# Linear attention with a gated product behind it: key features as the stationary side, and k of two heads projected in PSUM

## The chip, the cores and the metric

The kernel runs on one core of a Trainium2 chip. The metric is the device time of one execution in microseconds (us); the median of repeated runs counts.

## The reference

`phi` maps each token of a head (64 numbers) to 256 features; the attention is linear in them. Its output, with all heads of a token side by side, goes through two weight matrices whose products are multiplied, and through a third. q, k, v and w_phi are float32, the other three weights float64.

```python
# q, k, v: 8 batches, 8 heads, 576 tokens, 64 numbers; w_phi: 64 x 128
def phi(x):
    proj = np.einsum('bhsd,df->bhsf', x, w_phi)
    proj = proj - np.max(np.abs(proj), axis=-1, keepdims=True)
    return np.concatenate([np.exp(proj), np.exp(-proj)], axis=-1)
q_p, k_p = (phi(q), phi(k))
kv = np.einsum('bhsf,bhsd->bhfd', k_p, v)
z = np.sum(k_p, axis=2)
num = np.einsum('bhsf,bhfd->bhsd', q_p, kv)
den = np.einsum('bhsf,bhf->bhs', q_p, z)[..., None] + 1e-06
x = (num / den)               # then heads side by side: 4608 tokens x 512
a = x @ w_a                   # 512 x 1536
b = x @ w_b
return a * b @ w_out          # 1536 x 512
```

## The kernel before, in words

**Two parts that run woven into each other.** The attention goes over 32 pairs of heads (8 batches of 4 pairs; pair i is `b, pr = divmod(i, 4)`). The product behind it (called MoE in the names) goes over blocks of 288 tokens with the first 6 of 12 slices of the inner width (`moe_block`, lines 565 and 588), and then in a second pass over blocks of 512 tokens with the other six (`second_pass`, lines 648 and 695). `attention_steps` gives each stage of a pair a turn by a table of numbers (`K_TURNS`, `KV_TURN`, `Q_TURNS` and so on), and between turns `run` puts in steps of MoE blocks whose input is ready. Each tile comes from a pool with a fixed number of buffers, and the framework then sets the order of instructions on each engine and the waits.

**Precision.** An f32 matmul is slow, and an fp32r matmul rounds its inputs. So most products are made of split operands: a high part (rounded to fp32r) and a low part (what is left), and `products` multiplies high by high, high by low and low by high. The first pairs use plain f32 matmuls instead, which need no splitting by VectorE and ScalarE: `PLAIN_K` is the pair from which k is split for its projection, `PLAIN_KV` that from which the features and v are split, `PLAIN_NUM` and `PLAIN_Q` the same for the numerator and the queries.

**The keys of a pair.** `k_load` and `rest_load` fetch k and v: 512 tokens of two heads as four chunks of 128 tokens, and the remaining 64 tokens of two pairs together as one "rest" chunk. For plain pairs `features` multiplies a chunk (both heads' 64 numbers on 128 partitions) with `wk32`, a block-diagonal `w_phi` of 256 columns, into one tile `pk`. For split pairs k is loaded twice, so that each head's high part and low part lie one under the other on 128 partitions (`ks`, made by `stack`); one matmul per head with `wk2` of 256 columns (high `w_phi` twice, and its low part beside it) then gives two halves of `pk` that have to be added: ScalarE copies one half to `kb`, VectorE adds the other into `kd` (lines 236 and 237). VectorE takes the maximum (239) and subtracts it (240), ScalarE makes both exponentials `ke`, and `split` makes `keh` and `kel`.

**Sum over the tokens.** `kv_add` (line 292) accumulates v's transposed product with the features over all chunks in `kvps`: v with a column of ones is the stationary side (65 columns: `vaug` is v's high part with the ones, `vl` its low part), the features of one head (256 columns) are the moving side. In split pairs that is three matmuls per head and chunk. `k_finish` copies the sum (`kvT`), turns it by four TensorE transposes into `pt` (314), and makes `kvh` and `kvl`, which `q_side` uses for the numerators `pn` (370).

**PSUM.** The eight banks: three for the MoE (`ps_moe`), four that `pk`, `pq` (queries' projection) and `pn` share (`att`), one for `kvps` and `pt` (`kvacc`; batch 0 uses a bank of the MoE's).

Of the kernel before, what the change touches and what calls it, by code (L numbers as in the profile page):

```python
# [10 lines left out]
F32 = mybir.dt.float32  # L11
# [26 lines left out]
PLAIN_K, PLAIN_Q, PLAIN_KV, PLAIN_NUM = 9, 9, 11, 9  # L38
# [4 lines left out]
    "k_lo": "vvv",  # L43
    "v_hi": "sss",
# [15 lines left out]
def tile_kernel(ctx, tc, qT, km, kr, vm, vr, w_phi, w_a, w_b, w_out, out):  # L60
# [23 lines left out]
    TS = (HALF, T2)  # L84
    NFS = (SLICES0, DF // P - SLICES0)
# [25 lines left out]
    def attention_consts(a1):  # L111
# [7 lines left out]
        wk32 = a1.tile([P, 2, F], F32, tag="rk", name="wk32")  # L119
        nc.vector.memset(wk32, 0.0)  # L120
        for j in range(2):
            rows = slice(j * D, (j + 1) * D)
            nc.vector.tensor_copy(wk32[rows, j, :], w2[rows, :])
        wk2 = a1.tile([P, 2, F], F32R, name="wk2")
        nc.vector.memset(wk2.bitcast(F32), 0.0)
        nc.vector.tensor_copy(wk2[:, 0, :], wh)
        nc.vector.tensor_copy(wk2[:D, 1, :], wl[:D])
# [28 lines left out]
    def k_load(b, pr, a1, a2, ps, consts, st):  # L156
# [4 lines left out]
        if i < PLAIN_K:  # L161
            k32 = a1.tile([P, n], F32, tag="ks", bufs=2, name=f"k32_{u}")
            nc.sync.dma_start(k32, km[b, pr])
        else:
            k32 = a1.tile([P, 2, n], F32, tag="k32", name=f"k32_{u}")
            for r in range(2):
                nc.sync.dma_start(k32[r * D : (r + 1) * D], km[b, pr].rearrange("(j d) s -> d j s", j=2))
        if i < PLAIN_KV:
            v32 = a1.tile([P, NFULL, 2, D + 1], F32, tag="vl", bufs=2, name=f"v32_{u}")
            nc.vector.memset(v32[:, :, :, D : D + 1], 1.0)  # L170
        else:
            v32 = a1.tile([P, NFULL, 2, D], F32, tag="v32", name=f"v32_{u}")
# [3 lines left out]
        if i >= PLAIN_K:  # L176
            ks = a1.tile([P, 2, n], F32R, tag="ks", bufs=2, name=f"ks_{u}")
            stack(ks, k32, engine("k_hi", b), engine("k_lo", b))
            st["k", b, pr] = (ks,)
        yield  # L180
        st["v", b, pr] = (v32,)
        if i >= PLAIN_KV:
            va = vaug[pr % 2]
            vl = a1.tile([P, NFULL, 2, D + 1], F32R, tag="vl", bufs=2, name=f"vl_{u}")
            split(va[:, :, :, :D], vl[:, :, :, :D], v32, engine("v_hi", b), engine("v_lo", b))
            st["v", b, pr] = (va, vl)
        yield

    def rest_load(b, g, a1, a2, ps, consts, st):
# [3 lines left out]
        if i < PLAIN_K:  # L193
            k32 = a1.tile([P, P], F32, tag="rk32", name=f"rk32_{u}")
            nc.sync.dma_start(k32, kr[b, g])
        else:
            k32 = a1.tile([P, 2, P], F32, tag="rk32", name=f"rk32_{u}")
            for r in range(2):
                nc.sync.dma_start(k32[r * D : (r + 1) * D], kr[b, g].rearrange("(j d) s -> d j s", j=2))
# [17 lines left out]

    def features(u, i, k_, c0, n, a2, ps, consts):

        wk32, wk2 = consts[3:5]  # L220
        d = a2.tile([P, 4, F], F32, tag="kd", bufs=1, name=f"kd_{u}")[:, : 2 * n]
        if i < PLAIN_K:
            pk = ps.tile([P, 2, 2 * F], F32, tag="att", name=f"pk_{u}")
            for c in range(n):
                nc.tensor.matmul(pk[:, c], k_[:, (c0 + c) * P : (c0 + c + 1) * P], wk32, start=True, stop=True)
            p = pk[:, :n].rearrange("p c (j f) -> p (c j) f", j=2)
        else:

            p = d
            kb = a2.tile([P, 4, F], F32, tag="kb", bufs=1, name=f"kb_{u}")  # L230
            for c in range(n):
                pk = ps.tile([P, 2, 2, F], F32, tag="att", name=f"pk_{u}_{c}")
                for j in range(2):
                    nc.tensor.matmul(pk[:, j], k_[:, j, (c0 + c) * P : (c0 + c + 1) * P], wk2, start=True, stop=True)  # L234
                to = slice(2 * c, 2 * c + 2)
                nc.scalar.copy(kb[:, to], pk[:, :, 1])
                nc.vector.tensor_tensor(d[:, to], pk[:, :, 0], kb[:, to], op=ALU.add)
# [20 lines left out]
    def k_chunks(b, pr, c0, a1, a2, ps, consts, st):  # L258

        u = f"{b}_{pr}"  # L260
        gen = features(f"{u}_{c0}", b * NPAIR + pr, st["k", b, pr][0], c0, 2, a2, ps, consts)
# [23 lines left out]
    def kv_add(b, pr, vs, es, st):  # L285

        left = st["kv_left", b, pr] = st["kv_left", b, pr] - 1
        for j in range(2):
            parts = products(vs, es)
            for n_, (v_, e_) in enumerate(parts):  # L290
                width = D if n_ == 2 else D + 1
                nc.tensor.matmul(  # L292
                    st["kv_ps", b, pr][:width, j],
                    v_[:, j, :width],
                    e_[:, j],
                    start=(left == NFULL and j == 0 and n_ == 0),
                    stop=(left == 0 and n_ == len(parts) - 1),
                    skip_group_check=True,
                )

    def spare(b, ps):

        return (ps_moe, "moe", 3) if b == 0 else (ps, "kvacc", 1)

    def k_finish(b, pr, a1, a2, ps, consts, st):
# [3 lines left out]
        kvT = a2.tile([P, 4, F], F32, tag="kb", bufs=1, name=f"kvT_{u}")  # L309
        nc.scalar.copy(kvT[: D + 1], st["kv_ps", b, pr][: D + 1].rearrange("p j (s f) -> p (j s) f", s=2))  # L310
        pool, tag, bufs = spare(b, ps)
        pt = pool.tile([P, 4, P], F32, tag=tag, bufs=bufs, name=f"pt_{u}")
        for g in range(4):
            nc.tensor.transpose(pt[:, g, : D + 1], kvT[: D + 1, g, :], ident[: D + 1, : D + 1])
# [527 lines left out]
```

## Time and profile before

| | |
|---|---|
| median of 3 runs | 1260.65 us (1260.07 to 1265.03) |
| span of the profiled execution | 1260.6 us |
| TensorE busy | 1229.8 us (98%) |
| weight loads busy (beside matmuls) | 1131.8 us (90%) |
| VectorE busy | 928.8 us (74%) |
| ScalarE busy | 734.3 us (58%) |
| GpSimd busy | 157.3 us (12%) |
| mean granted TensorE clock | 0.998 |

How to read the profile: PE is TensorE's matmul, PEld its weight load, which runs beside matmuls, DVE is VectorE, ACT ScalarE, POOL GpSimd, SP the queue that issues DMAs. A group's row gives line, engine, operation, output and inputs by the program's names, the shape (for a matmul "128*65 128x256": 128 partitions by 65 stationary columns, 256 moving columns), how often, busy us and mean ns of one, and then idle time before it with what ended it. A row of the timeline gives start, length and the group. The matmuls of the split pairs are fp32r though the rows print "f32".

### The profile page before, as it was taken

Reading aid. Unit: us, or ns where it says so; the run is one execution under the profiler, and the core shown is the slowest. Engines: PE = TensorE matmul, PEld = TensorE weight load, DVE = VectorE, ACT = ScalarE, POOL = GpSimd, SP = SyncE. Lnnn points to the kernel's source line nnn. Section 1 sums busy time; section 2 is a strip of 40 time slices with the busy share of each in tenths; the row PEclk is TensorE's granted clock in tenths of the full one; section 3 lists DMA queues with packets and bytes.
Section 4 is the critical chain, followed back from the end, with each engine's and each line's share of the span. In section 5 each row is a group of like instructions: output and inputs, shape, how many; then the busy total and the mean of one; then the engine's idle time right before and its main releaser. Section 6 shows DMA issues by size and latency. Waiting matters only on the chain.

```text
span 1260.6 us, 22965 instructions
## 1 busy us (share of the span) xinstructions
PE 1229.8 (98%) x8588; PEld 1131.8 (90%) x8588; DVE 928.8 (74%) x1682; ACT 734.3 (58%) x1577; POOL 157.3 (12%) x70
## 2 busy tenths in 40 slices
PE   7889999999999999999999999999999999999998
PEld 4556789899999999999999999999999999999997
DVE  6989658898898989989974983599556556456443
ACT  5766668788888889988885542454223223233221
POOL 2232221221222212221220000000000000000000
PEclk9999999999999999999999999999999999999999
DMA  7665443443444435344233561142432332331221
GB/s 188 174 182 154 117 125 90 108 128 103 122 110 123 127 101 141 81 129 130 62 82 104 166 204 58 46 146 83 125 94 70 107 101 67 101 103 51 66 68 50
DMA packets 126287, 138.24 MB, mean 110 GB/s; under 512 B 39712, under 2 KB 92448, under 8 KB 126176
## 3 DMA queue, kind: packets, MB, share of 16 engines
q1 hardware_dynamic: 126176, 136.78, 38.4%
q8 instruction: 67, 1.10, 0.4%
q14 instruction: 44, 0.36, 0.1%
HBM read 108.12 MB, written 28.61 MB: 108 GB/s over the span
## 4 chain that ended last, share of the span: by engine, by line
PE 76%; DVE 9%; DMA 6%; ACT 5%; issue 2%; SPq 1%; POOL 0%; DVEq 0%; ACTq 0%
PE pab L648 21%; PE po L695 11%; PE pa L565 10%; PE pb L565 10%; PE po L588 9%; PE kvps L292 6%; PE pn L370 5%; PE pq L346 2%; DMA raw_b<-in_w_b 1%; PE pk L234 1%; DVE qs L154 1%; DMA rb<-rec 1%; DMA r<-den 1%; DVE kd L240 1%; DVE kel L149 1%
## 5 line engine op out<-in xcount | busy, mean ns | idle before, releaser
L350 POOL PARTITION_ALL_REDUCE mb<-p x64 | 156.6, 2448 | 495.9 <-ACT p L347 465.8
L565 PE MATMUL pb<-xh,wh_b 128*128 128x288 f32 x384 | 114.9, 299 | 2.9 <-ACT h L569 2.9
L565 PE MATMUL pa<-xh,wh_a 128*128 128x288 f32 x384 | 115.5, 301 | 0.4 <-ACT o L591 0.2
L565 PE MATMUL pb<-xh,wl_b 128*128 128x288 f32 x384 | 114.5, 298 | 0.0
L565 PE MATMUL pa<-xh,wl_a 128*128 128x288 f32 x384 | 114.4, 298 | 0.0
L142 ACT CAST hh<-h 128x288 fp32r<-128x288 f32 (+1 forms) x150 | 72.7, 503 | 70.7 <-DVE h L570 40.7
L565 PE MATMUL pa<-xl,wh_a 128*128 128x288 f32 x384 | 113.2, 295 | 0.0
L565 PE MATMUL pb<-xl,wh_b 128*128 128x288 f32 x384 | 112.7, 293 | 0.0
L588 PE MATMUL po<-hh,wl_o 128*128 128x288 f32 x384 | 112.4, 297 | 0.0
L588 PE MATMUL po<-hl,wh_o 128*128 128x288 f32 x384 | 111.9, 295 | 0.3 <-DVE hl L149 0.3
L588 PE MATMUL po<-hh,wh_o 128*128 128x288 f32 x384 | 110.3, 298 | 0.6 <-DVE h L570 0.6
L149 DVE TENSOR_TENSOR hl<-h,hh 128x288 fp32r<-128x288 f32 (+1 forms) x150 | 81.2, 554 | 22.7 <-ACT hh L142 22.5
L695 PE MATMUL po<-hl,wh_o 128*128 128x512 f32 x216 | 84.5, 391 | 0.0
L695 PE MATMUL po<-hh,wl_o 128*128 128x512 f32 x216 | 84.3, 390 | 0.0
L533 DVE TENSOR_TENSOR x<-x,rb 128x288 f32<-128x288 f32 (+1 forms) x100 | 56.0, 564 | 37.8 <-DMA x<-xun 26.2
L695 PE MATMUL po<-hh,wh_o 128*128 128x512 f32 x216 | 79.2, 392 | 0.0
L565 PEld LDWEIGHTS pb<-xh,wh_b 128*128 128x128 f32 x384 | 72.2, 188 | 5.0 <-ACT h L569 3.9
L565 PEld LDWEIGHTS pa<-xh,wh_a 128*128 128x128 f32 x384 | 72.2, 188 | 3.8 <-issue 2.3
L588 PEld LDWEIGHTS po<-hl,wh_o 128*128 128x128 f32 x384 | 72.5, 189 | 1.1 <-DVE hl L149 0.7
L565 PEld LDWEIGHTS pa<-xl,wh_a 128*128 128x128 f32 x384 | 72.9, 190 | 0.6 <-issue 0.2
L565 PEld LDWEIGHTS pa<-xh,wl_a 128*128 128x128 f32 x384 | 72.1, 188 | 1.3 <-issue 1.1
L565 PEld LDWEIGHTS pb<-xl,wh_b 128*128 128x128 f32 x384 | 72.8, 190 | 0.3
(226 smaller groups left out, 3793.7 us busy)
## 6 DMA issues: line engine op xcount, KB each, us to landing
q<-in_qT SPq DMA_DIRECT2D x110, 144.0 KB
k<-in_km SPq DMA_DIRECT2D x55, 256.0 KB
xun<-xn SPq DMA_DIRECT2D x64, 144.0 KB
x<-xun SPq DMA_DIRECT2D x64, 144.0 KB
rb<-rec SPq DMA_DIRECT2D x128, 72.0 KB
part<-o SPq DMA_DIRECT2D x16, 576.0 KB
o<-part SPq DMA_DIRECT2D x36, 256.0 KB
out_x<-o SPq DMA_DIRECT2D x36, 256.0 KB
```

The lines of the kernel that those rows point to most:

```text
L142: eng.copy(dst, src)
L149: eng_lo.tensor_tensor(lo, src, hi, op=ALU.subtract)
L154: eng_lo.tensor_tensor(hi_lo[D:], src[D:], hi_lo[D:], op=ALU.subtract)
L292: nc.tensor.matmul(st["kv_ps", b, pr][:width, j], v_[:, j, :width], e_[:, j], start=(left == NFULL and j == 0 and n_ == 0), stop=(left == ...
L346: nc.tensor.matmul(pq[:, :HALF], w_, q_[:, tok], start=(n_ == 0), stop=(n_ == len(parts) - 1))
L350: nc.gpsimd.partition_all_reduce(mb, p32, P, bass_isa.ReduceOp.absmax)
L370: nc.tensor.matmul(pn[: D + 1, :HALF], kv_[:, 2 * j + s, :], e_[:, s, tok], **at)
L533: nc.vector.tensor_tensor(x32, x32, rb, op=ALU.mult)
L565: nc.tensor.matmul(acc, w[:, cc * P : (cc + 1) * P], x, start=(k == 0), stop=(k == 3 * NCC - 1))
L588: nc.tensor.matmul(acc, w[:, cc * P : (cc + 1) * P], h, start=(k == 0), stop=(k == 3 * NFS[p] - 1))
L648: nc.tensor.matmul(acc[to][:, i], w_, x_, skip_group_check=True, **at)
L695: nc.tensor.matmul(acc[cc], w[:, cc * P : (cc + 1) * P], h, **at)
```

## The change

The sides of `kv_add` are exchanged for split pairs: 128 features are now the stationary side (high and low part, for exp(x) and for exp(-x): four loads per head and chunk), and `vaug` is the moving side with 130 columns (`VW`): 64 of v's high part, one of ones, 64 of its low part, and one of zeros that makes the number even. The sum then lies with the features on partitions, so `k_finish` needs no transposes for these pairs; it adds the two parts of the columns (ScalarE copies one, VectorE adds the other, line 315 of the changed kernel) and splits the result. The two heads have a bank each, so `kvacc` has two banks, and `att` three instead of four.

k is split as it is loaded, once, into `kh` and `kl` of 512 columns; `features` multiplies with block-diagonal `wkh` and `wkl` in three matmuls per chunk that add up in PSUM, so that the copy to `kb` and the addition to `kd` go away and both chunks lie in one tile `pk`. `PLAIN_K` goes from 9 to 6 and `PLAIN_KV` from 11 to 8: three more pairs of each kind are split.

```diff
-PLAIN_K, PLAIN_Q, PLAIN_KV, PLAIN_NUM = 9, 9, 11, 9
+PLAIN_K, PLAIN_Q, PLAIN_KV, PLAIN_NUM = 6, 9, 8, 9
...
+    VW = 2 * D + 2
...
-        ps = c.enter_context(tc.tile_pool(name="ps_att", bufs=4, space=PSUM))
+        ps = c.enter_context(tc.tile_pool(name="ps_att", bufs=3, space=PSUM))
...
+        for wk, w in ((wk32, w2), (wkh, wh), (wkl, wl)):
+            nc.vector.memset(wk.bitcast(F32), 0.0)
+            for j in range(2):
+                rows = slice(j * D, (j + 1) * D)
+                nc.vector.tensor_copy(wk[rows, j, :], w[rows, :])
...
-            k32 = a1.tile([P, 2, n], F32, tag="k32", name=f"k32_{u}")
-            for r in range(2):
-                nc.sync.dma_start(k32[r * D : (r + 1) * D], km[b, pr].rearrange("(j d) s -> d j s", j=2))
+        k32 = a1.tile([P, n], F32, tag="k32", bufs=2, name=f"k32_{u}")
+        nc.sync.dma_start(k32, km[b, pr])
...
-            ks = a1.tile([P, 2, n], F32R, tag="ks", bufs=2, name=f"ks_{u}")
-            stack(ks, k32, engine("k_hi", b), engine("k_lo", b))
+            kh, kl = (a1.tile([P, n], F32R, tag=f"k{p}", bufs=2, name=f"k{p}_{u}") for p in "hl")
+            split(kh, kl, k32, engine("k_hi", b), engine("k_lo", b))
...
-            vl = a1.tile([P, NFULL, 2, D + 1], F32R, tag="vl", bufs=2, name=f"vl_{u}")
-            split(va[:, :, :, :D], vl[:, :, :, :D], v32, engine("v_hi", b), engine("v_lo", b))
+            split(va[:, :, :, :D], va[:, :, :, D + 1 : VW - 1], v32, engine("v_hi", b), engine("v_lo", b))
...
-                pk = ps.tile([P, 2, 2, F], F32, tag="att", name=f"pk_{u}_{c}")
-                for j in range(2):
-                    nc.tensor.matmul(pk[:, j], k_[:, j, (c0 + c) * P : (c0 + c + 1) * P], wk2, start=True, stop=True)
-                to = slice(2 * c, 2 * c + 2)
-                nc.scalar.copy(kb[:, to], pk[:, :, 1])
-                nc.vector.tensor_tensor(d[:, to], pk[:, :, 0], kb[:, to], op=ALU.add)
+        pk = ps.tile([P, 2, 2 * F], F32, tag="att", name=f"pk_{u}")
+        parts = products(k_, (wk32,) if len(k_) == 1 else (wkh, wkl))
+        for c in range(n):
+            tok = slice((c0 + c) * P, (c0 + c + 1) * P)
+            for n_, (x_, w_) in enumerate(parts):
+                at = dict(start=(c == n_ == 0), stop=(n_ == len(parts) - 1))
+                nc.tensor.matmul(pk[:, c], x_[:, tok], w_, skip_group_check=True, **at)
...
-            parts = products(vs, es)
-            for n_, (v_, e_) in enumerate(parts):
-                width = D if n_ == 2 else D + 1
-                nc.tensor.matmul(
-                    st["kv_ps", b, pr][:width, j],
-                    v_[:, j, :width],
-                    e_[:, j],
...
+            for s in range(2):
+                for n_, e_ in enumerate(es):
+                    at = dict(start=(left == NFULL and s == n_ == 0), stop=(left == 0 and n_ == 1))
+                    nc.tensor.matmul(acc[j][:, s, :VW], e_[:, j, s, :], vs[0][:, j], skip_group_check=True, **at)
...
-        return (ps_moe, "moe", 3) if b == 0 else (ps, "kvacc", 1)
+        return (ps_moe, "moe", 3) if b == 0 else (ps, "kvacc", 2)
...
+            kv = a2.tile([P, 4, D + 1], F32, tag="kb", bufs=1, name=f"kv32_{u}")
+            for j in range(2):
+                to = slice(2 * j, 2 * j + 2)
+                nc.scalar.copy(kv[:, to], acc[j][:, :, D + 1 : VW])
+                nc.vector.tensor_tensor(kv[:, to], acc[j][:, :, : D + 1], kv[:, to], op=ALU.add)
```

The order on TensorE, in the sum over the second half of pair 3 of batch 4 (`kvps_3`, features `keh_3_2` and `kel_3_2`), into which matmuls of the next pair's projection (`pk_0`) fall. Before:

```order
L292 MATMUL kvps_3_4802<-keh_3_2_4818,vaug_122 65x256
L292 MATMUL kvps_3_4802<-kel_3_2_4819,vaug_122 65x256
L292 MATMUL kvps_3_4802<-keh_3_2_4818,vl_3_4366 64x256
L234 MATMUL pk_0_2_0_4876<-wk_111,ks_0_4599 128x256 x2
L292 MATMUL kvps_3_4802<-keh_3_2_4818,vaug_122 65x256
L234 MATMUL pk_0_2_1_4881<-wk_111,ks_0_4599 128x256 x2
```

The same place in the changed kernel:

```order
L223 MATMUL pk_0_0_4917<-wkl,kh_0_4754 128x256
L223 MATMUL pk_0_0_4917<-wkh,kl_0_4755 128x256
L289 MATMUL kvps_3_1_4957<-vaug_127,kel_3_2_4978 128x130
L289 MATMUL kvps_3_1_4957<-vaug_127,keh_3_2_4977 128x130
L289 MATMUL kvps_3_1_4957<-vaug_127,kel_3_2_4978 128x130
L289 MATMUL kvps_3_0_4956<-vaug_127,keh_3_2_4977 128x130
```

The rows name the output's partitions and columns: 65 or 64 by 256 became 128 by 130, in two tiles, and `pk` has three kinds of products in one tile where it had one kind in two tiles.

On VectorE, where the projection of the next pair (batch 5, pair 0) is turned into `kd`. Before:

```order
L237 TENSOR_TENSOR kd_0_0_4758<-pk_0_0_0_4760,kb_0_0_4759 128x256
L237 TENSOR_TENSOR kd_0_0_4758<-pk_0_0_1_4765,kb_0_0_4759 128x256
L149 TENSOR_TENSOR kel_3_2_4819<-ke_3_2_4815,keh_3_2_4818 128x1024
L239 TENSOR_REDUCE m_0_0_4770<-kd_0_0_4758 128x4
L381 TENSOR_SCALAR r_1_4746<-r_1_4746 128x9
```

In the changed kernel:

```order
L226 TENSOR_REDUCE m_0_0_4924<-pk_0_0_4917 128x4
L351 TENSOR_TENSOR p_4_6_4829<-p_4_6_4829,mb_6_4908 128x576
L155 TENSOR_TENSOR qel_4_4728<-qe_4_4724,qeh_4_4727 128x1152
L227 TENSOR_TENSOR kd_0_0_4916<-pk_0_0_4917,m_0_0_4924 128x512
L155 TENSOR_TENSOR vaug_127<-v_5_1_4849,vaug_127 128x8x64
L315 TENSOR_TENSOR kv_4_3_5114<-kvps_3_0_4956,kv_4_3_5114 128x130
```

The two additions are gone, maximum and difference read PSUM, and the addition of `kvps`' two parts is new.

More of the change, by code (lines that the diff above doesn't have):

```diff
@@ L43 @@
     "k_lo": "vvv",
+    "kv_hi": "sss",
     "v_hi": "sss",
@@ L131, in attention_consts, with va_consts @@
         for i in range(2):
-            t = a1.tile([P, NFULL, 2, D + 1], F32R, name=f"vaug{i}")
-            nc.vector.memset(t[:, :, :, D : D + 1].bitcast(F32), 1.0)
+            t = a1.tile([P, NFULL, 2, VW], F32R, name=f"vaug{i}")
+            va_consts(t)
             vaug.append(t)
-        return w2, wh, wl, wk32, wk2, ident, vaug
+        return w2, wh, wl, wk32, (wkh, wkl), ident, vaug
+    def va_consts(t):
+        nc.vector.memset(t[..., D : D + 1].bitcast(F32), 1.0)
+        nc.vector.memset(t[..., VW - 1 : VW].bitcast(F32), 0.0)
     def engine(step, b):
@@ L192, in rest_load @@
         i = b * NPAIR + 2 * g
[L193 to L199, printed above, removed]
+        k32 = a1.tile([P, P], F32, tag="rk32", name=f"rk32_{u}")
+        nc.sync.dma_start(k32, kr[b, g])
         v32 = a1.tile([P, 2, D + 1], F32, tag="rv32", name=f"rv32_{u}")
@@ L260, in k_chunks @@
         u = f"{b}_{pr}"
[L261 removed]
+        gen = features(f"{u}_{c0}", b * NPAIR + pr, st["k", b, pr], c0, 2, a2, ps, consts)
         yield next(gen)
@@ L266, in k_chunks @@
             pool, tag, bufs = spare(b, ps)
-            st["kv_ps", b, pr] = pool.tile([P, 2, 2 * F], F32, tag=tag, bufs=bufs, name=f"kvps_{u}")
+            if b * NPAIR + pr < PLAIN_KV:
+                st["kv_ps", b, pr] = pool.tile([P, 2, 2 * F], F32, tag=tag, bufs=bufs, name=f"kvps_{u}")
+            else:
+                st["kv_ps", b, pr] = [
+                    pool.tile([P, 2, 2 * F], F32, tag=tag, bufs=bufs, name=f"kvps_{u}_{j}") for j in range(2)
+                ]
             st["kv_left", b, pr] = NFULL + 1
@@ L308, in k_finish @@
         assert st["kv_left", b, pr] == 0
[L309 to L314, printed above, removed]
         plain = b * NPAIR + pr < PLAIN_NUM
         kvh = a2.tile([P, 4, D + 1], F32 if plain else F32R, tag="kvh", name=f"kvh_{u}")
-        nc.scalar.copy(kvh, pt[:, :, : D + 1])
+        acc = st["kv_ps", b, pr]
+        if b * NPAIR + pr < PLAIN_KV:
+            kvT = a2.tile([P, 4, F], F32, tag="kb", bufs=1, name=f"kvT_{u}")
+            nc.scalar.copy(kvT[: D + 1], acc[: D + 1].rearrange("p j (s f) -> p (j s) f", s=2))
+            pool, tag, bufs = spare(b, ps)
+            pt = pool.tile([P, 4, P], F32, tag=tag, bufs=bufs, name=f"pt_{u}")
+            for g in range(4):
+                nc.tensor.transpose(pt[:, g, : D + 1], kvT[: D + 1, g, :], ident[: D + 1, : D + 1])
+            kv = pt[:, :, : D + 1]
+        else:
+            kv = a2.tile([P, 4, D + 1], F32, tag="kb", bufs=1, name=f"kv32_{u}")
[3 more added lines that the diff above has]
+                nc.vector.tensor_tensor(kv[:, to], acc[j][:, :, : D + 1], kv[:, to], op=ALU.add)
         st["kv", b, pr] = (kvh,)
-        if not plain:
+        if plain:
+            nc.scalar.copy(kvh, kv)
+        else:
             kvl = a2.tile([P, 4, D + 1], F32R, tag="kvl", name=f"kvl_{u}")
-            nc.vector.tensor_tensor(kvl, pt[:, :, : D + 1], kvh, op=ALU.subtract)
+            split(kvh, kvl, kv, engine("kv_hi", b), nc.vector)
             st["kv", b, pr] = (kvh, kvl)
```

61 lines of the change are left out of this document (22 added, 39 removed).

## Prediction

> **What bounds the kernel now.** The page's busy line and its chain of work come first: TensorE is busy 98% of the span, and it holds three quarters of the chain.
>
> ```profile
> PE 1229.8 (98%) x8588; PEld 1131.8 (90%) x8588; DVE 928.8 (74%) x1682; ACT 734.3 (58%) x1577; POOL 157.3 (12%) x70
> PE 76%; DVE 9%; DMA 6%; ACT 5%; issue 2%; SPq 1%; POOL 0%; DVEq 0%; ACTq 0%
> ```
>
> A busy share is a mean over stages, so next the busy time by stage. The stages' borders come from two tiles' rows: the split `pk`, which the change touches, starts at 148.6 us, and the last numerator `pn` of the attention at 681 us (their last two times are first and last start). The two rows behind them are busy time by stretch: its length, then PE, PEld, DVE, ACT, POOL.
>
> ```profile
> L234 PE MATMUL pk<-wk,ks x184: 275/281/497, 148.6 to 644.0; 128*128 128x256 f32 x184
> L370 PE MATMUL pn<-qeh,kvl x184: 288/294/344, 198.0 to 681.0; 128*65 128x288 f32 x184
> ...
> 0.00:150.00 150.00, 132.99 (x610) 85.44 (x611) 120.46 (x234) 98.30 (x213) 43.11 (x23) 0.99 0.61 165
> 150.00:700.00 550.00, 543.10 (x4061) 520.10 (x4060) 470.97 (x785) 452.41 (x978) 114.18 (x47) 1.00 0.41 112
> ```
>
> From 150 to 700 us TensorE (first busy number) stands still for 550.0 - 543.1 = 6.9 us only, while VectorE has 79 us free and ScalarE 98. So what the change gives VectorE and ScalarE can return at most those 6.9 us there, and what it does to the sum of TensorE's instructions goes into the end time nearly one to one. The clock in that stage is granted in full (1.00). The question is therefore one sum over TensorE's stream. Counts come from the groups by shape; an f32 matmul leaves two records, an fp32r one (both read "f32" here) leaves one.
>
> ```profile
> L292 PE MATMUL kvps<-keh,vaug 128*65 128x256 f32 x168 | 47.0, 280 | 0.0
> L292 PE MATMUL kvps<-kel,vaug 128*65 128x256 f32 x168 | 46.9, 279 | 0.0
> L292 PE MATMUL kvps<-keh,vl 128*64 128x256 f32 x168 | 46.9, 279 | 0.0
> L292 PE MATMUL kvps<-keh_r,rvh 64*65 64x256 f32 x40 | 12.0, 301 | 0.0
> L292 PE MATMUL kvps<-ke,v 128*65 128x256 f32 x176 | 44.2, 391 | 0.0
> L292 PE MATMUL kvps<-ke_r,rv 64*65 64x256 f32 x48 | 13.1, 389 | 0.0
> L234 PE MATMUL pk<-wk,ks 128*128 128x256 f32 x184 | 35.0, 289 | 0.0
> L234 PE MATMUL pk_r<-wk,rk 128*128 128x256 f32 x22 | 4.4, 281 | 0.0
> L225 PE MATMUL pk<-wk,k 128*128 128x256 f32 x72 | 20.3, 411 | 5.0 <-DMA k<-in_km 5.0
> L225 PE MATMUL pk_r<-wk,rk 128*128 128x256 f32 x10 | 3.0, 384 | 0.0
> L314 PE MATMUL pt<-ident,kvT 65*128 65x65 f32 x128 | 13.4, 227 | 3.9 <-ACT kvT L310 3.9
> ```
>
> The mean ns of one is a latency and not a price, because matmuls overlap. The price is the step from one start to the next, which the timeline gives (start, length, then the group; "x4" is four in a row):
>
> ```profile
> 120.66 1.89 PE L292 MATMUL kvps<-ke,v 128*65 128x256 f32 x8
> 122.38 1.03 PE L225 MATMUL pk<-wk,k 128*128 128x256 f32 x4
> ...
> 500.87 0.40 PE L234 MATMUL pk<-wk,ks 128*128 128x256 f32 x2
> 501.11 0.30 PE L565 MATMUL pb<-xh,wh_b 128*128 128x288 f32 x1
> ...
> 505.97 0.30 PE L565 MATMUL pb<-xh,wl_b 128*128 128x288 f32 x1
> 506.11 0.41 PE L314 MATMUL pt<-ident,kvT 65*128 65x65 f32 x4
> 506.32 0.38 PE L565 MATMUL pa<-xh,wh_a 128*128 128x288 f32 x1
> 506.54 0.29 PE L565 MATMUL pa<-xl,wh_a 128*128 128x288 f32 x1
> ...
> 509.59 0.28 PE L292 MATMUL kvps<-keh,vaug 128*65 128x256 f32 x1
> ...
> 510.88 0.28 PE L292 MATMUL kvps<-keh,vl 128*64 128x256 f32 x1
> ```
>
> - f32, 256 columns: 8 records in 1.72 us, so 0.215 a record and 0.430 a matmul.
> - fp32r `pk`, 256 columns: 2 in 0.24, so 0.120.
> - fp32r `kvps`, 256 columns: the two rows are the first and the last of twelve, 11 steps in 1.29 us, so 0.117.
> - Transposes: from 505.97 to 506.54 is 0.57 us; two matmuls of 288 columns alone would take 2 x 0.135 (0.120 x 288/256), so the four cost 0.30, or 0.075 each.
>
> **The change, part by part.** How many matmuls of each kind there are is counted in the two programs' orders.
>
> *What TensorE runs before:* `pk` in fp32r 184 + 22 = 206 x 0.120 = 24.7 us; `pk` in f32 (72 + 10)/2 = 41 x 0.430 = 17.6; `kvps` in fp32r 3 x (168 + 40) = 624 x 0.117 = 73.0; `kvps` in f32 (176 + 48)/2 = 112 x 0.430 = 48.2; transposes 128 x 0.075 = 9.6. Together 173.1 us.
>
> *And after:* `pk` in fp32r 351 x 0.120 = 42.1 (three products instead of two for each 128 tokens, and pairs 6 to 8 too); `pk` in f32 27 x 0.430 = 11.6; `kvps` in f32 80 x 0.430 = 34.4 (pairs 8 to 10 leave it); transposes 32 x 0.075 = 2.4; and 960 matmuls of the new form, 128 stationary columns against 130 moving ones, at an unknown step s. Together 90.5 us + 960 s.
>
> So all hangs on s, and the change breaks even at (173.1 - 90.5)/960 = 0.086 us. By moving columns alone it would win: 520 columns in four matmuls take the place of 768 in three. But the new form turns the sides round: the stationary side grows from 65 columns to 128, and each load serves 130 columns only. What a load costs is seen where nothing hides it. At 179.71 us TensorE has just stood idle; its rows, and then those of the weight loads:
>
> ```profile
> 179.71 0.40 PE L346 MATMUL pq<-qs,wh 128*128 128x288 f32 x1
> 179.95 0.29 PE L346 MATMUL pq<-qs,wl 128*128 128x288 f32 x1
> ...
> 179.71 0.19 PEld L346 LDWEIGHTS pq<-qs,wh 128*128 128x128 f32 x1 [0.39 <-DVE vl L149]
> 179.82 0.19 PEld L346 LDWEIGHTS pq<-qs,wl 128*128 128x128 f32 x1
> ```
>
> The second load starts 0.11 us after the first, although it need not wait for any matmul's end; and the first matmul takes 0.24 us to the next, not 0.135: the other 0.105 is its own load, exposed. The mean lengths of loads say the same:
>
> ```profile
> L234 PEld LDWEIGHTS pk<-wk,ks 128*128 128x128 f32 x184 | 27.9, 189 | 1.3 <-issue 0.9
> L292 PEld LDWEIGHTS kvps<-keh,vaug 128*65 128x65 f32 x168 | 22.7, 135 | 0.2 <-issue 0.2
> L314 PEld LDWEIGHTS pt<-ident,kvT 65*128 65x128 f32 x128 | 12.4, 142 | 6.4 <-ACT kvT L310 4.3 <-POOL mb L350 1.3 <-issue 0.4
> ```
>
> 63 more columns take 189 - 135 = 54 ns more, 0.86 ns a column; 128 columns take 0.110 us. A load of 128 columns is just covered by 256 moving columns (step 0.120). It isn't by 130, which are worth 130 x 0.120/256 = 0.061 us. So the new matmuls should run at the pace of their loads: s between 0.105 (the exposed load above) and 0.120 (the step that 128 stationary columns have now, where 256 moving ones may set it too). I take s = 0.112, near the 0.110 of the lengths and of the two loads' starts, with a little for the handing over.
>
> At s = 0.112: 90.5 + 107.5 = 198.0 us, **24.9 us more** than 173.1. At 0.105 it is 18.2 more, at 0.120 it is 32.6 more.
>
> The Trainium skill has a rule that gives another sum. Its page "TensorE: Matmul & The Clock Gate", section "Back-to-back issue gap", puts the sustained step of load and matmul pairs at about 81 ns for 128 moving columns; by it 960 x 0.081 = 77.8, and the change would save 4.8 us. The rows above speak against it for this type, since two loads of 128 fp32r columns start 0.11 us apart; but no run shows the new form yet.
>
> *VectorE and ScalarE.* Gone are the copies and adds that joined the two heads' `pk`, and the work on `ks` at 1024 columns:
>
> ```profile
> L237 DVE TENSOR_TENSOR kd<-pk,kb 128x256 f32<-128x256 f32 x92 | 35.5, 415 | 7.4 <-ACT kb L236 6.5 <-ACT ke_r L249 0.5
> L236 ACT COPY kb<-pk 128x256 f32<-128x256 f32 x92 | 31.5, 383 | 2.8 <-PE pk L234 2.8
> L154 DVE TENSOR_TENSOR ks<-k,ks 64x1024 fp32r<-64x1024 f32 x23 | 28.1, 1223 | 0.7
> ```
>
> Back come 26 differences `kl` of 512 columns (half of L154's, so some 0.6 us each, 16 us), 48 adds of 130 columns in the end of a pair (half of L237's, some 0.21 us, 10 us), and three more pairs' splits of the features. Both engines get lighter by 30 us or so each. It is worth nothing at the end beyond TensorE's 6.9 us of idle time, of which I count none: the new form waits for the same `kel` as the old.
>
> *DMA.* For the split pairs each `km` comes once instead of twice (55 issues of this tensor become 32). No wait for `km` stands in TensorE's list after the first at 5.0 us, which stays. Nothing.
>
> *PSUM.* The ring that `pk`, `pq` and `pn` share goes from four banks to three. Up to 700 us the wait for a bank to come free shows as
>
> ```profile
> PE pq L346 <- ACT xn L371: 1.9, 2, 1.1
> ```
>
> two waits, 1.9 us in all. The ring also gets fewer tiles: `pk` needs one bank for two chunks where it needed two (per pair 2.25 instead of 4.5, beside eight of the queries). Between zero and a few us; I take zero, and for the upper end 10 us, ten waits like these.
>
> *After 700 us* nothing is changed; that stage starts later by what the first lost.
>
> **Sum.** 1260.6 + 24.9 = 1285.5 us. The profiled execution's span, 1260.6, is the median of the runs shown (1260.65), so nothing is added for what lies around it.
>
> **The rivals.**
>
> *The short matmul is cheap after all (faster).* The transposes load 128 columns as well, with only 65 moving, and (0.41 - 0.227)/3 = 0.061 us is the step from one to the next. Were the new loads as quick, s = 0.061 would be set by the 130 columns: 90.5 + 58.6 = 149.1, 24.0 us less: 1237. It decides below s = 0.086. Against it: the transposes' load is 142 ns long and the fp32r load of as many columns 189, so the transposes load in a way of their own. 0.07.
>
> *Loads half hidden (no change).* If a load overlaps in part with the load before it, s lies between 0.061 and 0.110, in the middle about 0.086, which gives 1260; 5 ns to either side make it 1255 to 1265. It needs two fp32r loads of 128 columns closer than 0.11 us, and the rows at 179.71 show them not closer. 0.06. (The skill's 81 ns, named above, would be such a step, at 1256.)
>
> *Fp32r loses its rate on short matmuls (far slower).* Every fp32r matmul in this trace moves 256 columns or more; none shows that 130 go at the same rate. If they fell back to the f32 rate, 0.430 x 130/256 = 0.218 us: 90.5 + 209.3 = 299.8, 126.7 more: 1387. For it speaks only that nothing excludes it. 0.13.
>
> *PSUM's third bank is missed.* As forecast, plus one wait of 1 us (the row's 1.9/2) for every tenth of some 240 tiles in the ring, 24 us: 1310. Against it, the ring gets fewer tiles. 0.06.
>
> **How the numbers follow.** The forecast has 0.68, and its own range is 1260.6 + 18.2 - 6.9 = 1272 to 1260.6 + 32.6 + 10 = 1303. The whole range goes down to 1255 for the half-hidden loads and up to 1310 for the banks; what is left out (0.07 and 0.13) is 0.20. Half a per cent, 6.3 us, is about what a measurement here can tell from no change. Faster: 0.07, and 0.01 of the half-hidden case: 0.08. Same: the rest of that and a forecast nearly eaten up by returned idle time: 0.06. Slower: 0.86.
>
> **What would show it.** In the changed profile the rows of `kvps` with 130 columns should follow each other at about 0.112 us, and their loads as well, so that loads and not matmuls set the pace; `pk` should still step at 0.12 with half as many matmuls again; the joins L236 and L237 should be gone, and VectorE and ScalarE lighter from 150 to 700 us with TensorE's idle time there no larger than now. The stage that ends at 680 us should end some 25 us later, and the last 560 us should look alike. I am wrong if the 130-column rows step at 0.06 to 0.08 (then it is faster or the same) or above 0.2 (then it is 100 us slower), or if TensorE waits for `pn`, `pq` or `pk` banks by more than 10 us.

## The result, and the profile after

The changed kernel takes 1282.34 us (median of 4 runs, 1281.34 to 1283.29), the kernel before on the same chip 1262.84 (1260.07 to 1266.55): a ratio of 1.0154, with a 95% interval of 1.0124 to 1.0184. It is slower, and near the forecast of 1285.5. The profiled execution has a span of 1280.1 us where the one before had 1260.6, so 19.5 us are to be explained where the sum gave 24.9. One run of the kernel p_bounds below took 3056.50 us, far from its six others, and is left out of its numbers.

The profile page's busy line and its chain of work:

```profile
PE 1257.5 (98%) x8881; PEld 1166.8 (91%) x8881; DVE 897.7 (70%) x1671; ACT 712.0 (56%) x1516; POOL 157.1 (12%) x70
PE 91%; DMA 4%; DVE 3%; ACT 1%; SPq 1%; issue 1%; DVEq 0%; ACTq 0%
```

TensorE's busy time grew by 1257.5 - 1229.8 = 27.7 us, and the time in which it stands still shrank by 8.2, from 30.8 to 22.6 (span less busy time). 27.7 - 8.2 = 19.5. VectorE and ScalarE are 31 and 22 us lighter. On the chain, TensorE's share rose from 76% to 91%. The stages' busy times (length, PE, PEld, DVE, ACT, POOL, granted clock):

```profile
0.00:150.00 150.00, 133.24 (x611) 85.35 (x611) 125.04 (x247) 100.50 (x217) 41.00 (x22) 0.98 0.56 158
150.00:700.00 550.00, 549.38 (x4193) 534.12 (x4193) 437.28 (x767) 426.51 (x911) 116.06 (x48) 1.00 0.37 101
```

From 150 to 700 us TensorE now stands still for 0.6 us instead of 6.9. The disputed rows come next: the new sum's matmuls in the timeline (start, length, group), and then the loads that belong to them.

```profile
499.80 0.38 PE L289 MATMUL kvps<-rva,kel_r 64*128 64x130 f32 x2
500.02 0.27 PE L289 MATMUL kvps<-rva,keh_r 64*128 64x130 f32 x1
500.23 0.48 PE L370 MATMUL pn<-qeh,kvh 128*65 128x288 f32 x2
...
501.27 0.28 PE L289 MATMUL kvps<-vaug,kel 128*128 128x130 f32 x1
501.38 0.28 PE L289 MATMUL kvps<-vaug,keh 128*128 128x130 f32 x1
...
502.05 0.28 PE L289 MATMUL kvps<-vaug,keh 128*128 128x130 f32 x1
```

```profile
501.21 0.19 PEld L289 LDWEIGHTS kvps<-vaug,kel 128*128 128x128 f32 x1
501.32 0.19 PEld L289 LDWEIGHTS kvps<-vaug,keh 128*128 128x128 f32 x1
...
501.99 0.19 PEld L289 LDWEIGHTS kvps<-vaug,keh 128*128 128x128 f32 x1
```

From 501.27 to 502.05 are seven steps, from one start to the next, 0.111 us each; the loads go from 501.21 to 501.99 in seven steps as well, the same 0.111. The matmuls follow their loads. The groups' rows, by contrast, show nothing of it: 269 ns for one is its latency.

```profile
L289 PE MATMUL kvps<-vaug,keh 128*128 128x130 f32 x384 | 87.7, 269 | 0.0
L289 PE MATMUL kvps<-vaug,kel 128*128 128x130 f32 x384 | 86.0, 269 | 0.0
L315 DVE TENSOR_TENSOR kv<-kvps,kv 128x130 f32<-128x130 f32 x48 | 12.8, 280 | 4.1 <-ACT kv L314 4.1
L155 DVE TENSOR_TENSOR kl<-k,kh 128x512 fp32r<-128x512 f32 x26 | 17.8, 684 | 0.0
```

One row speaks against a step of the prediction: the last split numerator `pn` (last two times: first and last start) is not later but earlier than the 681.0 of before.

```profile
L370 PE MATMUL pn<-qeh,kvl x184: 288/294/299, 204.5 to 670.2; 128*65 128x288 f32 x184
```

The loss stands in how much of the MoE was left over by then. These are the rows of `pa`, `pb` and `po` from 150 to 700 us, one tile after the other (busy time and count of TensorE alone); of before:

```profile
150.00:700.00 550.00, 119.62 (x760) 1.00 0.41 112
150.00:700.00 550.00, 119.35 (x756) 1.00 0.41 112
150.00:700.00 550.00, 117.48 (x787) 1.00 0.41 112
```

and of the changed kernel:

```profile
150.00:700.00 550.00, 117.86 (x720) 1.00 0.37 101
150.00:700.00 550.00, 114.74 (x709) 1.00 0.37 101
150.00:700.00 550.00, 109.39 (x720) 1.00 0.37 101
```

That is 2303 matmuls before and 2149 after: 154 matmuls of 288 columns, at 0.135 us each 21 us of work, left for the time after 700 us. There TensorE's busy time grew by as much, from 553.7 to 574.9 us.

### The profile page after: what moved, and what is told of

It is laid out like the page before. It is cut to its first block, busy times and chain, and to the rows that moved or that the text cites. A ratio compares the mean times of both kernels' runs of the same rounds, so it can differ in the third digit from the quotient of the medians.

```text
span 1280.1 us, 23404 instructions
## 1 busy us (share of the span) xinstructions
PE 1257.5 (98%) x8881; PEld 1166.8 (91%) x8881; DVE 897.7 (70%) x1671; ACT 712.0 (56%) x1516; POOL 157.1 (12%) x70
## 4 chain that ended last, share of the span: by engine, by line
PE 91%; DMA 4%; DVE 3%; ACT 1%; SPq 1%; issue 1%; DVEq 0%; ACTq 0%
PE pab L648 21%; PE pa L565 12%; PE pb L565 12%; PE po L588 12%; PE po L695 11%; PE kvps L289 9%; PE pn L370 8%; PE pk L223 3%; PE pq L346 3%; DMA raw_a<-in_w_a 2%; PE kvps L284 1%; DMA raw_b<-in_w_b 1%; DMA r<-den 0%; PE pk_r L223 0%; DVE p L351 0%
## 5 line engine op out<-in xcount | busy, mean ns | idle before, releaser
L155 DVE TENSOR_TENSOR hl<-h,hh 128x288 fp32r<-128x288 f32 (+1 forms) x150 | 84.9, 577 | 28.6 <-ACT hh L148 28.3
L289 PE MATMUL kvps<-vaug,keh 128*128 128x130 f32 x384 | 87.7, 269 | 0.0
L289 PE MATMUL kvps<-vaug,kel 128*128 128x130 f32 x384 | 86.0, 269 | 0.0
L570 DVE TENSOR_TENSOR h<-pb,h 128x288 f32<-128x288 f32 x96 | 43.5, 453 | 48.0 <-PE pb L565 42.2
```

The source lines that it names most:

```text
L155: eng_lo.tensor_tensor(lo, src, hi, op=ALU.subtract)
L289: nc.tensor.matmul(acc[j][:, s, :VW], e_[:, j, s, :], vs[0][:, j], skip_group_check=True, **at)
L570: nc.vector.tensor_tensor(h32, pab["b"], h32, op=ALU.mult)
```

## The experiments

Two theories stood against each other at first. The first: the pace of the loads makes the new sum dear, and TensorE's sum of prices is the time. The second: prices matter less than waits (the missing bank, the lighter engines, the boundaries). The first table gives times, each against runs of the kernel before on the same chip (the chips differ from table row to table row, so small differences between rows are better read from each row's distance to its own "before"); the second what their profiles show. "Idle" is span less busy time of TensorE, "clock" the span times what the mean granted clock lacks of 1 (both from each profile's heads; the clock is given to 0.001, so an entry is good to some 0.6 us), and the last column is the last start of the split `pn`.

| kernel | us | before there | ratio, 95% interval |
|---|---|---|---|
| p_bounds (six runs) | 1266.29 | 1260.65 | 1.0043, 1.0025 to 1.0060 |
| k_proj | 1272.85 | 1260.65 | 1.0095, 1.0079 to 1.0111 |
| v_kv | 1299.63 | 1260.65 | 1.0312, 1.0290 to 1.0334 |
| dead_join | 1286.74 | 1260.65 | 1.0216, 1.0191 to 1.0241 |
| wide256 | 1295.14 | 1262.65 | 1.0259, 1.0241 to 1.0278 |
| narrow66 | 1291.91 | 1262.65 | 1.0227, 1.0207 to 1.0248 |
| half64 | 1248.51 | 1262.65 | 0.9893, 0.9872 to 0.9915 |
| att3 | 1276.28 | 1262.65 | 1.0118, 1.0091 to 1.0144 |
| k_att3 | 1267.50 | 1261.01 | 1.0054, 1.0035 to 1.0073 |
| old_bounds | 1282.70 | 1261.01 | 1.0175, 1.0158 to 1.0192 |

| profile | span | PE busy | idle | clock | last `pn` |
|---|---|---|---|---|---|
| before | 1260.6 | 1229.8 | 30.8 | 2.5 | 681.0 |
| after | 1280.1 | 1257.5 | 22.6 | 3.8 | 670.2 |
| p_bounds | 1263.5 | 1233.0 | 30.5 | 12.6 | 696.1 |
| k_proj | 1270.6 | 1246.5 | 24.1 | 5.1 | 639.2 |
| v_kv | 1301.4 | 1258.4 | 43.0 | 19.5 | 758.8 |
| dead_join | 1284.0 | 1259.0 | 25.0 | 7.7 | 735.5 |
| wide256 | 1293.4 | 1269.0 | 24.4 | 5.2 | 682.9 |
| narrow66 | 1289.8 | 1263.1 | 26.7 | 14.2 | 680.7 |
| half64 | 1251.6 | 1225.5 | 26.1 | 10.0 | 674.4 |
| att3 | 1273.6 | 1236.1 | 37.5 | 8.9 | 730.6 |
| k_att3 | 1267.0 | 1241.7 | 25.3 | 6.3 | 686.6 |
| old_bounds | 1280.3 | 1257.7 | 22.6 | 7.7 | 671.4 |

**The moving side: wide256.** The changed kernel with 256 moving columns instead of 130.

```diff
-nc.tensor.matmul(acc[j][:, s, :VW], e_[:, j, s, :], vs[0][:, j], ...)
+v_ = vs[0].rearrange("p j w -> p (j w)")[:, 4 * j : 4 * j + 256]
+nc.tensor.matmul(acc[j][:, s], e_[:, j, s, :], v_, ...)
...
```

> The changed kernel with 256 moving columns instead of 130 in the exchanged sum (the tile holds both heads' columns side by side; the 126 further columns are computed and not used). Load-pace theory: the step goes from 0.112 to the 0.120 that 128 stationary and 256 moving columns have elsewhere: 960 x 0.008 = 8 us slower than the changed kernel. Rival (a load and its matmul add up, 0.051 and 0.061): the step becomes 0.17, 56 us slower.

Twice the moving columns cost 1295.14 - 1282.34 = 12.8 us over 960 matmuls, where the load-pace theory had 8 and its rival 56. The step, in the timeline:

```profile
509.05 0.28 PE L290 MATMUL kvps<-vaug,keh 128*128 128x256 f32 x1
...
509.65 0.28 PE L290 MATMUL kvps<-vaug,kel 128*128 128x256 f32 x1
```

Five steps in 0.60 us: 0.120 instead of 0.111. So 126 more columns cost 0.009 us, where at the pace of the columns they would cost 0.059; they fit beside the load. At 960 matmuls that is 8.6 us; of the other 4 us the table has 1.8 as idle time and 1.4 in the clock column, and the step doesn't explain them.

**narrow66.** The changed kernel with 66 moving columns: v's low part is left out of the sum.

```diff
-nc.tensor.matmul(acc[j][:, s, :VW], e_[:, j, s, :], vs[0][:, j], ...)
+nc.tensor.matmul(acc[j][:, s, : D + 2], e_[:, j, s, :], vs[0][:, j, : D + 2], ...)
...
```

> The changed kernel with 66 moving columns instead of 130: the products with v's low part are left out (all but one column), and the addition at the end of a pair reads neighbouring columns instead. Load-pace theory: the step stays 0.110 to 0.112 and the time within 3 us of the changed kernel. Rival (moving columns set or share the step): 64 columns x 0.00047 x 960 = 29 us faster.

Half the moving columns shorten no step that waits for its load. The timeline shows both what a load costs and what it hides:

```profile
506.11 0.46 PE L370 MATMUL pn<-qeh,kvh 128*65 128x288 f32 x2
506.40 0.19 PE L289 MATMUL kvps<-vaug,kel 128*128 128x66 f32 x1
506.43 0.28 PE L289 MATMUL kvps<-vaug,keh 128*128 128x66 f32 x1
506.54 0.28 PE L289 MATMUL kvps<-vaug,kel 128*128 128x66 f32 x1
...
507.10 0.28 PE L289 MATMUL kvps<-vaug,keh 128*128 128x66 f32 x1
```

Behind two numerators, which left time for the loads, the first of these matmuls takes 0.03 us; from 506.43 on each waits for its load, six steps in 0.67 us, 0.112 each. So the load sets the pace here too. But the kernel is 9.6 us slower than the changed one, which neither theory has. The table puts 14.2 - 3.8 = 10.4 us of it to the clock: seven stretches of half clock, four of them between 300 and 580 us, where the other kernels have none or one. The timeline shows such a stretch coming and going, and the stretches' rows give the granted clock (0.57):

```profile
309.15 0.28 PE L289 MATMUL kvps<-rva,kel_r 64*128 64x66 f32 x1
309.36 0.61 PE L565 MATMUL pa<-xh,wh_a 128*128 128x288 f32 x1
309.76 0.44 PE L565 MATMUL pa<-xl,wh_a 128*128 128x288 f32 x1
310.00 0.44 PE L565 MATMUL pa<-xh,wl_a 128*128 128x288 f32 x1
...
312.64 0.36 PE L565 MATMUL pb<-xh,wh_b 128*128 128x288 f32 x1
312.85 0.29 PE L565 MATMUL pb<-xl,wh_b 128*128 128x288 f32 x1
```

```profile
309.00:313.00 4.00, 4.00 (x20) 3.91 (x20) 3.48 (x12) 3.06 (x9) 0.00 (x0) 0.57 0.23 45
313.00:353.00 40.00, 40.00 (x316) 39.55 (x314) 33.03 (x52) 32.18 (x68) 8.95 (x4) 1.00 0.38 104
353.00:357.00 4.00, 4.00 (x20) 3.93 (x20) 3.14 (x12) 3.82 (x10) 0.00 (x0) 0.59 0.37 85
```

For some 3.4 us matmuls step at 0.24 instead of 0.13 us, while the busy share reads 4.00 of 4.00. The last matmul ahead of it belongs to a series of the smallest ones (64 rows, 66 columns); so it is at all four places (last one at 309.15, 352.92, 526.68, 571.66 us; half clock from 309.3, 353.7, 527.9, 572.2). Other such series have no such stretch behind them, so the series alone doesn't decide it.

**The stationary side: half64.** The changed kernel with 64 of the 128 stationary columns, in all chunks of a pair but the first: half the features are left out of the sum there.

```diff
+m_ = F if left == NFULL else F // 2
-nc.tensor.matmul(acc[j][:, s, :VW], e_[:, j, s, :], vs[0][:, j], ...)
+nc.tensor.matmul(acc[j][:m_, s, :VW], e_[:, j, s, :m_], vs[0][:, j], ...)
```

> The changed kernel with 64 stationary columns instead of 128 in all chunks of a pair but its first (768 of 960 matmuls; the other features' sums are left out there), the moving side as it is. Load-pace theory: the load falls to 0.055, the 130 moving columns (0.061) take over, step near 0.066: 768 x 0.046 = 35 us faster than the changed kernel, that is some 15 us faster than before. Rival (a fixed price per matmul of about 0.11, whatever the columns): no change.

The kernel takes 33.8 us less than the changed one (1248.51 against 1282.34), with the same number of matmuls and as many moving columns:

```profile
504.20 0.22 PE L290 MATMUL kvps<-vaug,keh 128*64 128x130 f32 x1
...
504.88 0.23 PE L290 MATMUL kvps<-vaug,kel 128*64 128x130 f32 x1
```

The load-pace theory had 35 us. Eleven steps in 0.68 us, 0.062 each: what 130 columns were worth in the prediction (0.061). So the load of the other 64 columns is what the change pays for.

**The boundaries alone: p_bounds.** The kernel before, with only the two pair numbers moved.

```diff
-PLAIN_K, PLAIN_Q, PLAIN_KV, PLAIN_NUM = 9, 9, 11, 9
+PLAIN_K, PLAIN_Q, PLAIN_KV, PLAIN_NUM = 6, 9, 8, 9
```

> The kernel before with only the two boundaries moved (PLAIN_K 6, PLAIN_KV 8). Load-pace theory, by the prediction's prices: on TensorE 14 f32 matmuls of pk (0.430) become 28 fp32r (0.120), 32 f32 of kvps become 96 fp32r (0.117): 2.7 + 2.5 = 5.2 us less; they lie between 100 and 230 us, where TensorE waits at times and VectorE and ScalarE get three more pairs of splits. So 0 to 5 us faster than before. Rival (the boundaries are what made the changed kernel slower, because the early stage is bound by VectorE and ScalarE): 5 to 15 us slower.

Prices say 5.2 us less (three pairs of each kind at fp32r rates); it is 5.6 us slower. That is the size that the rival named, but not its reason: in the profiled execution, 2.9 us longer than the one before, busy time rose by 3.2 us and idle time not at all, while the clock column rose by 10.1. That loss lies in the first 150 us, where the granted clock (third from the end) went from 0.99 to 0.93:

```profile
0.00:150.00 150.00, 133.86 (x606) 88.05 (x607) 129.01 (x247) 102.01 (x223) 38.65 (x22) 0.93 0.62 166
150.00:700.00 550.00, 540.74 (x4060) 519.10 (x4059) 475.23 (x781) 461.18 (x994) 117.59 (x48) 1.00 0.41 108
```

Six runs of it lie at a mean clock of 0.988 to 0.992, and twelve runs of the kernel before at 0.994 to 0.997, so the loss belongs to the program.

**The new projection alone: k_proj.** p_bounds with k split once, three products per chunk and both chunks in one `pk`; the sum as before. As in the change, `k32` of the split pairs has a second buffer.

```diff
-            ks = a1.tile([P, 2, n], F32R, tag="ks", bufs=2, name=f"ks_{u}")
-            stack(ks, k32, engine("k_hi", b), engine("k_lo", b))
+            kh, kl = (a1.tile([P, n], F32R, tag=f"k{p}", bufs=2, name=f"k{p}_{u}") for p in "hl")
+            split(kh, kl, k32, engine("k_hi", b), engine("k_lo", b))
...
```

> The kernel before with the boundaries moved and only the projection of k as in the changed kernel (three products added up in PSUM, no copy and add). Load-pace theory: 117 more matmuls x 0.120 = 14.0 us on TensorE against p_bounds, of which up to 6.9 us come back as idle time that the lighter VectorE and ScalarE no longer leave: 7 to 14 us slower than p_bounds. Rival (the projection is the loss and the sum is not): 20 us slower than p_bounds.

By prices it costs 14.0 us (117 more matmuls, 0.120 us each); against p_bounds it costs 6.6, a little less than the 7 to 14 expected. Idle time fell by 6.4 us and the clock column by 7.5. How much of the idle time is due to the joins that went away is the question of dead_join.

**The new sum alone: v_kv.** The changed kernel with the old projection of k, three banks in the ring.

```diff
-            kh, kl = (a1.tile([P, n], F32R, tag=f"k{p}", bufs=2, name=f"k{p}_{u}") for p in "hl")
-            split(kh, kl, k32, engine("k_hi", b), engine("k_lo", b))
+            ks = a1.tile([P, 2, n], F32R, tag="ks", bufs=2, name=f"ks_{u}")
+            stack(ks, k32, engine("k_hi", b), engine("k_lo", b))
...
```

> The changed kernel with the old projection of k (stacked ks, two matmuls, copy and add): against p_bounds only the sum over tokens has its sides exchanged. Load-pace theory: 960 x 0.112 - 720 x 0.117 = 23.3 us more, 96 transposes x 0.075 = 7.2 less: 16 us slower than p_bounds, 11 slower than before, and TensorE's idle time from 150 to 700 us stays near 7 us. Rival (the exchanged sum costs nothing, the third product of the projection is the loss): within 3 us of p_bounds or 7 faster.

It is the slowest of all: 33.3 us above p_bounds, where the price of the sum, and what was expected, is 16.1 (960 x 0.112 in place of 720 x 0.117 and 96 x 0.075). Idle time rose by 12.5 us and the clock column by 6.9. Something in it waits that doesn't in the changed kernel, and the bank was the suspect.

**The bank alone: att3.** The kernel before with three banks instead of four.

```diff
-        ps = c.enter_context(tc.tile_pool(name="ps_att", bufs=4, space=PSUM))
+        ps = c.enter_context(tc.tile_pool(name="ps_att", bufs=3, space=PSUM))
```

> The kernel before with three banks instead of four in the ring that pk, pq and pn share (one bank stays unused). Theory of the prediction: the ring has room, 0 to 3 us slower than before. Rival (the third bank is missed): waits of TensorE for pk, pq and pn grow by 10 us or more, and the time by 10 to 24 us.

The bank is worth 13.6 us, with not one instruction more on TensorE: 6.7 of idle time and 6.4 in the clock column. So the theory of the prediction is refuted for this kernel and the time is the rival's, but the rival's waits are not there. The idle time isn't where the bank is missed: from 150 to 700 us TensorE stands still for 5.1 us, less than before. The last `pn` starts at 730.6 us instead of 681.0, and from 718 us to then the timeline has no MoE matmul left to run beside the attention's tail. The rows of two stretches there:

```profile
700.00:720.00 20.00, 18.64 (x145) 17.84 (x144) 13.45 (x18) 13.87 (x29) 6.09 (x3) 1.00 0.30 86
720.00:740.00 20.00, 14.59 (x93) 12.92 (x94) 6.51 (x13) 8.53 (x17) 2.26 (x1) 0.91 0.34 98
```

That is 6.8 us of standing still in 40, and a clock of 0.91 in half of them; the kernel before stands still for 1.0 us there. The waits of TensorE after 690 us (total, times, longest) name the numerators' own inputs, which no other work covers now.

```profile
PE pn L370 <- ACT qeh L142: 4.3, 3, 1.7
PE pn L370 <- DVE qel L149: 2.0, 3, 0.7
```

The rest of the clock's loss falls in the first 150 us, where the granted clock is 0.95 instead of 0.99 (0.04 x 150 = 6 us, from rounded numbers). Why it should fall there with a bank less isn't shown.

**The bank under the new projection: k_att3.** k_proj with the same one-line edit.

> The kernel k_proj (new projection of k, old sum, boundaries at pairs 6 and 8) with three banks instead of four for the projections and numerators. TensorE's list of instructions is the same. Theory 1, the missing bank hurts only while pk takes 4.5 tiles of the ring for each pair, and the new projection takes 2.25: 1273 to 1277 us, 0 to 4 above k_proj, where the kernel before lost 13.6. Theory 2, the bank is missed as much with half the pk tiles, since the numerators hold the ring: 1283 to 1288.

1267.50, under the ranges of both theories: the missing bank costs nothing here, and the kernel is even 5 us faster than k_proj (ratios 1.0054 and 1.0095, intervals apart). The last `pn` starts at 686.6. So the new projection, with 2.25 tiles of the ring for each pair instead of 4.5, does without the bank. Whether that is due to the number of tiles or to the joins, which held each tile longer, isn't separated: the next run has as few tiles, and with the joins its attention ends late again. Why k_proj with its fourth bank is the slower of the two isn't shown: idle and clock are alike, and its busy time is 4.8 us more for the same instructions.

**The joins as dead work: dead_join.** The changed kernel, with a copy to `kb` and an addition to `kd` put back for split pairs; their result is overwritten.

```diff
...
+            for c in range(n):
+                to = slice(2 * c, 2 * c + 2)
+                nc.scalar.copy(kb[:, to], p[:, to])
+                nc.vector.tensor_tensor(d[:, to], p[:, to], kb[:, to], op=ALU.add)
```

> The changed kernel with the copy and the addition of the old join put back as dead work in each split projection (same ScalarE copy of 128x256 into kb and VectorE addition into kd, which the subtraction then overwrites): 117 copies and 117 additions, some 45 us on each of the two engines, nothing more on TensorE. Theory that the lighter engines gave back TensorE's idle time: idle from 150 to 700 us goes from 0.6 to 4 to 8 us and the time up by as much against the changed kernel. Rival (the idle time went because TensorE's longer stream covers the others): within 1.5 us of the changed kernel.

4.4 us slower than the changed kernel by medians, 6.6 when each is set against the kernel before on its own chip, 3.9 by spans: 2.4 us more of idle time, 3.9 more in the clock column, and 2.4 less of other busy time. The attention's end moved from 670 to 735 us, yet little of that reaches the end time, because the MoE's work fills in. So putting the joins back brings back 2.4 of the 8.2 us of idle time, not most of it. From 150 to 700 us TensorE stands still for 1.6 us instead of 0.6, below the 4 to 8 expected, and the time grew by more than the rival's 1.5: neither theory has it.

**The boundaries in the changed kernel: old_bounds.** Both are moved back, `PLAIN_KV` to 10 and not quite to the 11 of before.

```diff
-PLAIN_K, PLAIN_Q, PLAIN_KV, PLAIN_NUM = 6, 9, 8, 9
+PLAIN_K, PLAIN_Q, PLAIN_KV, PLAIN_NUM = 9, 9, 10, 9
```

> The changed kernel with the boundaries moved back: k is split from pair 9 on, features and v from pair 10 on. By matmul prices (three pairs' projection back in f32: 14 x 0.430 - 41 x 0.120 = +1.1 us; two pairs' sum back in f32: 21 x 0.430 + 8 transposes x 0.075 - 80 x 0.112 = +0.7) TensorE has 1.8 us more. Theory 1, the boundaries cost nothing by themselves: 1284 us (1282 to 1287). Theory 2, splitting earlier is what cost the kernel before its 5 us when its boundaries alone were moved (thin stretches and the half clock in the first 110 us), and the changed kernel pays that too: 1272 to 1278.

1282.70 us, the same as the changed kernel within the intervals (1.0175, 1.0158 to 1.0192, against 1.0154, 1.0124 to 1.0184). In this kernel the boundaries cost nothing that these runs can tell, and this run's second theory falls.

**The steps in a row.** Each against the kernel before on its own chip: boundaries +5.6, then the new projection +6.6, then the bank taken away -5.7, then the exchanged sum +13.0; together the 19.5 us. The exchange costs 16.1 by prices (from k_att3's instructions to the changed kernel's) and 13.0 as measured: in the profiles busy time grows by 15.8 us, as priced, and idle time shrinks by 2.7.

## Why the prediction was right, point by point

- *TensorE's stream is the bound.* Right: VectorE and ScalarE gave back 53 us of work (31 and 22, where some 30 each were forecast), and the kernel is slower by about what TensorE got. But it holds for the stream as a whole and not for each edit: k_att3 has 14 us more of matmuls than p_bounds and is within 1 us of its time, with 5.2 us less of idle time and 6.3 less in the clock column.
- *The step s of the new matmul.* Forecast 0.112 us at the pace of the loads; measured 0.111. The three products of `pk` step at 0.118 (517.72 to 518.31 us, five steps), as forecast. Both sides of the claim were tried: more moving columns ride along (0.120 at 256), fewer save nothing (0.112 at 66), and half the stationary columns halve it (0.062). The Trainium skill's page "TensorE: Matmul & The Clock Gate", section "Back-to-back issue gap", puts 128 moving columns at about 81 ns in a sustained stream; for these fp32r matmuls the trace disagrees, with 111 ns.
- *The sum, +24.9 us.* Busy time grew by 27.7 us, about 1 of it in the clock column: some 26.5 where 24.9 was worked out. The sum starts from a span, 1260.6, as if it were a run's time; a run's time is 1.7 to 2.1 us longer than its span (1281.83 against 1280.1 in the changed kernel's profiled run), so the 1285.5 is a span too, 5.4 us above the one measured.
- *"I count none" for TensorE's idle time.* This is the term that was mis-sized, and more than the whole of the miss of 5.4 us: idle time fell by 8.2 us, 6.3 of it from 150 to 700 us, where the prediction had named 6.9 as the most that could come back and took zero. The reason given, that the new form waits for the same `kel`, looked at one wait only. The projection's joins and the number of its tiles changed too: k_proj against p_bounds has 6.4 us less idle time with the old sum. Dead_join gives 2.4 of that kind to the joins. The rest is not shown apart: fewer tiles in the ring, the second buffer of `k32`, or TensorE's longer stream. Two kernels point to a share of the last: with joins and tiles as in the changed kernel and a longer stream (wide256) or a shorter one (half64), TensorE stands still from 150 to 700 us for 0.0 and 2.7 us, in the changed kernel for 0.6. Their rows:

```profile
150.00:700.00 550.00, 550.00 (x4125) 532.05 (x4124) 423.25 (x727) 420.08 (x893) 116.68 (x48) 1.00 0.34 95
150.00:700.00 550.00, 547.35 (x4426) 530.81 (x4425) 443.32 (x777) 430.04 (x930) 113.47 (x48) 1.00 0.37 103
```

- *PSUM, zero.* Right for the changed kernel: k_att3 loses nothing by the bank, and the changed kernel's one wait of the kind that the prediction counted (total, times, longest) comes to 1.8 us, where there were 1.9 before. The reason named, half as many `pk` tiles, fits, but the lighter joins would fit as well.

```profile
PE pk L223 <- ACT xn L371: 1.8, 1, 1.8
```

  But in the kernel before, the same bank is worth 13.6 us, above the upper end of 10 that came from ten waits like those, and in a way that the row of waits doesn't show: about half is paid in a tail of the attention that has no other work beside it, and the rest in the clock. The rival with the missed bank was probably real for the old projection: v_kv is 17.2 us above the price of its sum, of which the joins and the clock may have a share.
- *The boundaries.* They are 5.2 us less inside the sum. In the kernel before they cost 5.6, with 10 us more in the clock column; in the changed kernel moving them back makes no difference. That the changed kernel doesn't pay this was luck: nothing in the prediction looked at it.
- *"The stage that ends at 680 us should end some 25 us later, and the last 560 us should look alike."* Wrong: it ends at 670, and 154 MoE matmuls moved behind it. The prediction treated the stage as a fixed list; but the MoE's steps are woven in by turns, and the loss shows in what is left over.
- *The rivals.* The cheap short matmul and the half-hidden loads fell with s. That fp32r might lose its rate on short matmuls (0.13) fell as well: at 0.03 us for 66 columns behind a finished load (narrow66), and 0.062 for 130 (half64), the rate is that of 256 columns in 0.120 us.

## What to carry to other kernels

Before exchanging the two sides of a matmul, price both: the step is the larger of the time for the moving columns and that for loading the stationary ones, and a load of 128 fp32r columns (0.111 us here) is only covered by some 240 moving columns (an estimate: 0.111 over the 0.120/256 us of one column). Price a stream by steps from start to start, and test the bound by changing each side alone. A buffer that no wait names can still matter, by delaying one of two interleaved streams until the other has run out: look at when each stream ends, not only at the waits while both run.

## What the runs showed of the hardware that was not expected

- TensorE's clock falls to half for stretches of 3.4 us, or two or three times that (in v_kv the granted clock is 0.50 from 107.6 to 117.8 us), and it does so while the busy share reads 100%, as in narrow66. By the clock column the kernel before lost 2.5 us to it, v_kv 19.5. Behind series of matmuls of 64 rows by 66 columns it came four times in one kernel. How much is lost belongs to the program (p_bounds in all its runs), and what triggers it was not settled.
- Between matmuls that use 64 rows and those that use 128 there is a longer step: in the changed kernel's timeline above, two 64-row matmuls follow each other at 0.11 us (499.80 to 500.02 for two), and from the last of them to the 128-row `pn` it takes 0.21 (500.02 to 500.23). In narrow66's timeline the same change takes 0.21 (309.15 to 309.36), where its small matmuls step at 0.112.
- Two edits that each cost time in the old kernel, the bank (+13.6 us) and the projection's extra matmuls, cost next to nothing together: k_att3, which has both, stands 0.9 us from p_bounds, which has neither (6.5 and 5.6 us above the kernel before).

No version that computes the whole was faster than the kernel before.
